# Packing an attention output of 28-of-32 rows to 448 rows, and running FF2 and the output product in pairs of 64-row halves, in a fused attention and MLP kernel

## The chip, the cores and the metric

The kernel runs on one core of one Trainium2 chip. The metric is the device time of one execution in microseconds (us). The engines of a core work side by side, each through its own stream of instructions in order: TensorE (PE) multiplies matrices, VectorE (DVE), ScalarE (ACT) and GpSimd (POOL) work on elements, SyncE (SP) and POOL issue transfers here. They wait for each other by semaphores. A matmul has a stationary operand, loaded by an instruction of its own (PEld), and a moving one; the result adds up in one of eight banks of PSUM.

## The reference

```
x = A_x                                   # (1, 2048, 448), bf16
xn = layernorm(x)
q, k, v = split(xn @ wqkv)                # 16 heads of 28
o[p] = softmax over 8 keys p, p-2, ..., p-14 of (q[p] . k) / sqrt(28), times v
s = concat_heads(o) @ wo                  # 448 x 448
g = silu(gelu(xn @ w1 + b1) @ w2 + b2)    # 448 -> 1792 -> 448
out = x + s * g
```

A position attends to eight positions at a distance of two, itself and earlier ones, so even and odd positions never meet.

## The kernel before

The 2048 positions are 16 tiles of 128, in 4 chunks (`NCH`) of 4 tiles (`TPC`); the even positions and the odd ones are laid out one after the other. All weights stay in SBUF. The kernel is a list of tasks, each a few instructions on one engine, and a string `ORDER` (L17 on) that names every task once, with a letter for its engine (P, V, A, G for POOL, S for SP, D for the landing of a transfer). `emit` goes through that string and issues the tasks, so the order on every engine is written out by hand; no scheduler moves anything. Buffers come out of pools (`take`, `give`) in the same order, and a task waits for whatever its data and its buffer depend on.

The stages:

- LayerNorm: statistics on DVE (L332, L336), the normalised tile `xn` (L366), which is transposed to `xnT` by PE (L381) for the first tiles and by transfers issued on SP (`dma_T`, L279) for the others. x is loaded by SP in transfers of four tiles (`x_sb`).
- qk and v projection (L457, L481) and FF1 (L516). D = 448 is three and a half times 128 rows, so these contract 7 slices of 64 rows. `pair(a, b)` runs two such jobs side by side, one in the top 64 rows of PE's array and the other in the bottom 64: first 4 slices of each, then 3 more with the halves exchanged, each job into its own bank. Between the two parts stands a "told" nop (L416) on POOL or SP: it waits for the first part's matmuls, and the second part waits for it. FF1's bias b1 comes by a transfer on POOL and is turned by PE (L772).
- The evacuated q and k are transposed by transfers on SP into `qkT` (L279); v is copied by transfers on POOL (L273).
- Scores (L599), exp on ACT (L609), the band masks (built on POOL, L731 to L738, multiplied on DVE, L615), values (L631). DVE brings the values' output into `oT` (L641, L645, L650, L655): four groups of 32 rows (a group is a head slot), of which 28 hold data, times 4 slices. `wo` is loaded in the same shape by POOL, with zeros in the rows that nothing fills.
- FF2: `ff2_part`, 14 full matmuls (128 rows by 448 columns) for each tile into one bank (L550); then y = bank + b2 on DVE (L565), tanh on ACT (L577; silu from the table for the last chunk, L572), and g on DVE (L581). g waits in a ring of buffers, which grows by the qkv weights' buffers (`late_g`) once those are spent.
- The end of a tile: `final_part`, 4 full matmuls with `wo` (L685), times g (L691, L693), plus x (L699), store by SP (L703).

PE's work around the end is FF2 of the last chunk and the output products, the last tile in column parts of 336 and 112.

Of the kernel before, what the change touches and what calls it, by code (L numbers as in the profile page):

```python
# [17 lines left out]
D0 V1 G17 S34 D35 A36 D37 V15 V16 P2 V22 S38 D39 V23 G50 V24 G51 D52 V25 V26 P3 V27 V28 S44 D45 V29 V30 G31 V18 V19  # L18
G32 P4 V20 G33 V21 S40 D41 P5 A53 S42 D43 P6 G100 S46 D47 P7 V60 P8 S48 D49 P9 V61 S76 D77 V64 A62 P10 S78 D79 V63
P11 P12 V106 P13 S80 D81 P14 V107 P108 V65 P109 A66 V110 P132 V67 V113 V114 P115 V117 A111 V68 D112 P136 P116 A118  # L20
P133 V69 A70 V71 S82 D83 V120 V121 S86 D87 P190 G102 V72 V73 A74 D119 P137 S88 D89 S90 D91 V191 P134 P122 P123 V124
P135 P138 A139 D125 P149 G150 A143 G168 D169 V75 V126 V127 V140 P128 G170 D171 P129 V130 A148 A54 G172 D173 P151
V153 D131 P318 G319 A145 P163 A152 G174 D175 V101 P320 S141 D142 A144 A321 A322 G178 D179 P156 S154 D155 V84 G176
D177 P313 V96 G164 P165 V85 P333 V97 V94 V95 V92 A167 G99 V200 V204 G314 P315 A166 G334 V205 P335 A316 V201 S202
D203 G157 V93 G98 S206 D207 P158 V196 V197 G180 D181 S198 D199 G182 D183 V192 V193 A336 P308 S194 D195 V160 A159
G309 A317 S146 D147 S161 D162 G184 D185 P323 G324 G186 D187 G188 D189 A337 P310 A311 S272 D273 V290 P325 P328 A326
G246 D247 V291 A327 P227 G329 P330 V294 V295 A331 S274 D275 V299 P215 G252 D253 G280 D281 V303 A312 G228 P229 A230
A231 A332 S276 D277 G216 P217 V301 A219 P338 G339 P548 P340 G549 P550 P234 G235 A341 V103 A218 A551 P208 A342 G104
P236 A237 A238 A552 V105 V296 P538 V304 P543 G539 G544 S232 D233 V300 P540 A542 G209 P210 P553 G554 A211 P545 S278
D279 A212 P533 G534 S220 D221 V302 S213 D214 A546 A547 P555 V305 V306 G307 V423 V419 V427 A541 A557 V428 P528 G529  # L30
P558 G559 A556 P535 A537 V431 P530 A532 P560 S239 D240 V432 V297 P222 A561 A531 A536 S433 D434 V292 G223 P241 V424
S429 D430 A562 S425 D426 P224 G242 P243 V293 G298 A225 A55 P691 A692 V420 G248 D249 A698 V355 S421 D422 V356 S357
D358 A694 G282 D283 G284 D285 P508 P509 P568 P569 A226 A696 P513 P518 V695 V693 V697 P514 V510 G286 D287 V343 G288
D289 V699 G250 D251 V351 V352 A511 A244 V245 G254 D255 V512 V570 V347 V348 V344 A571 V572 P700 V701 P519 V515 A516
P727 A728 S345 D346 V520 G256 D257 A521 G258 D259 V702 G260 D261 V705 A730 V706 A734 V707 G262 D263 V703 S349 D350
P523 V704 A732 V708 P524 P709 G264 D265 S353 D354 V517 A712 P359 A716 G266 D267 S360 P378 V713 V525 V522 A526 P361
A714 S379 A363 P380 A381 P366 S367 V362 S364 D365 V729 V717 G268 D269 A710 V711 P385 P368 A370 V715 V369 A382 S371
D372 S383 G270 D271 D384 V735 G386 P387 V388 P718 A389 V719 V720 V721 S390 D391 V722 P853 P745 V854 P573 V855 A748
V723 V724 A752 V527 V731 V725 V726 A746 V733 P858 P563 V859 P564 V565 P574 V575 P863 A566 V567 S856 D857 P736 G397
D398 V864 V865 P454 P461 G401 D402 V747 A750 S455 P456 P442 V737 A457 A458 G462 V741 V742 P463 P449 V743 V744 G443  # L40
V738 V739 S866 D867 A465 P444 S459 D460 V751 A464 A446 P435 V740 G450 S466 D467 V749 S436 V445 P451 A452 A453 P468
P437 V860 G469 V753 P470 V472 P754 P868 A438 A439 V471 S440 D441 V869 P763 S447 D448 A766 A770 V870 S871 D872 V755
A768 V756 P873 V874 A764 V757 V758 P578 P579 V580 V759 P781 A784 V767 V760 A786 S861 D862 P373 A581 A782 P583 S374
P375 G584 A788 A377 A56 V376 G407 D408 G409 D410 G411 D412 P585 V761 P588 P593 S594 S589 V762 G399 D400 V787 A586
P392 G415 D416 G405 D406 V582 V875 P595 V785 V771 A587 G393 P603 P590 G403 D404 A596 V769 A591 P394 S876 D877 G473
V396 A592 A395 G413 D414 V765 G417 D418 S604 G474 D475 G476 D477 G478 D479 P605 A607 P608 A576 P613 A597 A606 V789
P772 V777 S614 S609 P610 G480 D481 G482 D483 A611 A612 G484 D485 G486 D487 V773 P598 S599 P615 P600 A617 V778 V774
V783 P790 V775 V776 P878 V779 A602 V791 V780 G490 D491 A601 G488 D489 G494 D495 A616 A57 V879 V795 G492 D493 V792
V793 V796 P888 P799 A800 V889 A806 A802 A804 V577 P618 P619 V794 V890 V807 P883 V884 V805 P817 A824 V620 A820 P628
P835 A838 V801 A818 V803 V797 V798 P629 P808 V813 A836 P893 G496 D497 G498 D499 V630 P633 V814 V815 A621 A840 P623  # L50
V816 V825 V885 V622 A631 V632 P624 P634 S891 D892 A842 G500 D501 A822 A58 P643 P648 S644 V894 V895 S896 D897 P645
V635 P663 V841 A636 V843 V880 S881 D882 G502 D503 G504 D505 S649 V809 V625 V810 V811 V812 V823 A646 V837 A626 A647
V839 P650 S664 V819 P665 P638 A667 A666 V821 P653 A652 S639 A651 P640 S654 G506 D507 V637 P655 A657 A656 V627 S886
D887 A641 P826 V827 P668 S669 V828 V831 P658 S659 V829 V830 P670 A671 A642 P660 A661 V832 A672 A662 A59 V833 V834
P844 P903 V904 V905 S906 D907 P898 V899 P908 V909 V910 S911 D912 P918 P913 V845 V846 V847 V900 S901 D902 V848 V849
V850 V851 V852 P673 P674 V675 P681 P682 P923 P677 P678 P685 V683 A676 V914 V915 S916 D917 A684 V924 V925 S926 D927
V679 A680 P686 V919 V920 A687 S921 D922 P928 V929 V930 P688 P689 A690 S931 D932 P933 V934 V935 S936 D937
# [61 lines left out]
def kernel(  # L119
# [13 lines left out]
    P = 128  # L133
# [34 lines left out]
    const = ctx.enter_context(tc.tile_pool(name="const", bufs=1))  # L168
    psum = ctx.enter_context(tc.tile_pool(name="psum", bufs=1, space=bass.MemoryType.PSUM))
# [11 lines left out]
    wo = sb("wo", [P, KT, D])  # L181
# [21 lines left out]
    p_xn = ring("xn", 4, [P, 512])  # L203
# [11 lines left out]
    p_g.bufs = p_g.bufs + late_g  # L215
# [46 lines left out]
    t_wo = [plan.add("POOL", memset("gpsimd", wo[:], 0.0), [t_on])]  # L262
# [141 lines left out]
    def pair(a, b, early=False):  # L404
        held = {}

        def part(j, ps, kt, half, n):
            return lambda: j.part(ps, kt, half, n == 0, n == 6)

        def f1(k):  # L410
            p, q = buf(p_b, k, 0), buf(p_b, k, 1)
            held["last"] = together([part(a, p, kt, 0, kt) for kt in range(4)], [part(b, q, kt, 1, kt) for kt in range(4)])[-1]
        t = plan.add("PE", f1, a.deps + b.deps + a.late + b.late, take=(p_b, p_b) + a.into + b.into)

        def f2(k):
            held["told"] = (nc.gpsimd if k.on == "POOL" else nc.sync).nop()  # L416
# [116 lines left out]

    def ff2(t):
        t_g[t] = []
        for cs, n, end in parts(t):
            ff2_part(t, cs, n, end)

    def ff2_part(t, cs, n, end):
# [18 lines left out]
        a = halves[1]  # L558
        t_f2[t] = a

        if biased:
            y, pool, held = halves[0], p_b, ((p_b, halves[0], 0),)
        else:
            def f2(k):
                nc.vector.tensor_tensor(out=buf(p_y, k)[:, :n], in0=buf(p_b, halves[0])[:, :n], in1=b2[:, cs], op=ALU.add)  # L565
            y, pool = plan.add("DVE", f2, [a, t_b2], take=(p_y,), give=((p_b, halves[0], 0),)), p_y
# [3 lines left out]
        if c == NCH - 1:  # L570
# [15 lines left out]
    t_oT = [[] for _ in range(NT)]  # L586

# [88 lines left out]

    def final(t):
# [3 lines left out]
    def final_part(t, cs, n, g):  # L681
        def f1(k):
            ps = buf(p_b, k)
            for kt in range(KT):
                nc.tensor.matmul(ps[:, :n], oT[:, kt, t * P:(t + 1) * P], wo[:, kt, cs],  # L685
                                 start=(kt == 0), stop=(kt == KT - 1))
        a = plan.add("PE", f1, t_oT[t] + t_wo, take=(p_b,))

        def f2(k):
            if t >= NT - TPC:  # L690
                nc.vector.tensor_tensor(out=buf(p_sg, k)[:, :n], in0=buf(p_b, a)[:, :n], in1=buf(p_g, g)[:, :n], op=ALU.mult)  # L691
                return
            nc.vector.scalar_tensor_tensor(out=buf(p_sg, k)[:, :n], in0=buf(p_b, a)[:, :n], scalar=0.5,  # L693
                                           in1=buf(p_g, g)[:, :n], op0=ALU.mult, op1=ALU.mult)
        s = plan.add("DVE", f2, [a, g], take=(p_sg,), give=((p_b, a, 0), (p_g, g, 0)))
# [142 lines left out]
```

## Time and profile before

| | us |
|---|---|
| median of three runs | 155.57 |
| the three runs | 154.44, 155.7, 155.57 |
| the profiled execution | 155.02 |
| its span in the profile | 153.3 |

The profiled execution has 5268 instructions and moves 17.36 MB. The span is the time between the first and the last instruction on the core; 1.7 us of the execution lie around it. In the views below times count from the span's start. A row of the chain gives a start, a length, the engine and the line; a row of a group gives its busy time and the mean of one instruction in ns. PE's matmuls are pipelined, so the mean of one (342 ns for L550) is longer than the distance between two.

### The profile page before, as it was taken

The numbers are of one execution on the slowest core, as the hardware profiler recorded it, in microseconds if no ns is written. First come the engines' busy times: TensorE is split into PE (matmuls) and PEld (weight loads), VectorE is DVE, ScalarE is ACT, GpSimd is POOL, SyncE is SP. The second block draws the span as 40 slices with busy tenths as digits, with TensorE's granted clock in tenths as the row PEclk, the third lists the DMA queues.
The fourth block names the chain that finished last, engine by engine and source line by source line (L and its number), as shares of the span: only waits on it lengthen the run. The fifth ranks groups of instructions, "written<-read, shape, count | busy, mean of one in ns | idle before, by whom it ended". The sixth has DMA issues, their size and how long they took to land.

```text
span 153.3 us, 5268 instructions
## 1 busy us (share of the span) xinstructions
PE 148.6 (97%) x2200; PEld 78.6 (51%) x2200; DVE 107.3 (70%) x273; ACT 89.0 (58%) x165; POOL 43.0 (28%) x95
## 2 busy tenths in 40 slices
PE   6999999999999999999999999999999999999991
PEld 2454555555555555555554554445555445455561
DVE  4688540029524959899997877549977895989842
ACT  3239577786797407842246549689658358670320
POOL 7805666040349234020000005389600000000000
PEclk9999999999999999999999999999999999999999
DMA  4999988999997844069317681323310010002012
GB/s 150 285 287 330 155 164 178 156 375 176 285 122 141 122 87 88 4 128 129 85 34 137 75 106 46 96 59 88 92 34 0 4 62 30 4 32 62 13 47 60
DMA packets 33575, 17.36 MB, mean 113 GB/s; under 512 B 25203, under 2 KB 32387, under 8 KB 33552
## 3 DMA queue, kind: packets, MB, share of 16 engines
q1 hardware_dynamic: 31472, 14.03, 44.4%
q0 software_dynamic: 1936, 2.88, 8.9%
q8 instruction: 17, 0.28, 0.8%
q10 hardware_dynamic: 144, 0.11, 0.2%
q14 instruction: 6, 0.05, 0.1%
HBM read 7.06 MB, written 1.84 MB: 58 GB/s over the span
## 4 chain that ended last, share of the span: by engine, by line
PE 97%; DVE 1%; issue 0%; ACT 0%
PE bank L550 28%; PE bank L516 28%; PE bank L457 14%; PE bank L685 8%; PE bank L481 7%; PE bank L599 4%; PE bank L631 4%; PE bank L245 3%; PE bank L381 1%; DVE xnT L232 0%; DVE sg L691 0%; ACT w_in L572 0%; DVE h L237 0%; DVE o L699 0%; PE bank L548 0%
## 5 line engine op out<-in xcount | busy, mean ns | idle before, releaser
L516 PE MATMUL bank<-xnT,w 64*128 64x512 bf16 x392 | 45.1, 376 | 0.0
L550 PE MATMUL bank<-w,h 128*128 128x448 bf16 (+2 forms) x238 | 44.7, 342 | 0.0
L520 ACT ACTIVATE h<-bank,b 128x512 bf16<-128x512 f32 x56 | 35.4, 689 | 11.2 <-PE bank L516 11.2
L273 POOL DMA_DIRECT2D v<-v_tok x52 | 27.3, 533 | 48.6 <-DVE v_tok L232 25.3
L550 PEld LDWEIGHTS <-h 128*128 128x128 bf16 x238 | 22.1, 98 | 18.9
L516 PEld LDWEIGHTS <-w 64*128 64x128 bf16 x392 | 20.4, 94 | 20.9 <-issue 0.8
L457 PE MATMUL bank<-w_in,xnT 64*128 64x448 bf16 (+1 forms) x212 | 24.8, 352 | 0.2 <-DVE xnT L232 0.2
L609 ACT ACTIVATE E<-bank 128x456 bf16<-128x456 f32 (+1 forms) x36 | 17.8, 549 | 10.0 <-PE bank L599 9.3
L332 DVE BATCH_NORM_STATS2 st<-x_sb 128x6 f32<-128x448 bf16 x16 | 9.5, 609 | 12.7 <-DMA x_sb<-in_A_x_dram 12.7
L641 DVE STREAM_TRANSPOSE dt<-bank 128x480 f32<-128x480 f32 (+1 forms) x18 | 11.8, 663 | 7.0 <-PE bank L631 3.8
L457 PEld LDWEIGHTS <-xnT 64*128 64x128 bf16 (+1 forms) x212 | 10.9, 94 | 9.5 <-DVE xnT L232 0.4
L577 ACT ACTIVATE t<-y 128x448 f32<-128x448 f32 x12 | 6.9, 576 | 15.0 <-DVE y L565 15.0
L685 PE MATMUL bank<-wo,oT 128*128 128x448 bf16 (+2 forms) x68 | 14.1, 342 | 0.0
L481 PE MATMUL bank<-w_in,xnT 64*128 64x448 bf16 (+1 forms) x106 | 13.7, 352 | 0.0
L650 DVE STREAM_TRANSPOSE dt<-rd 128x480 f32<-128x480 f32 (+1 forms) x18 | 11.9, 666 | 0.3
L655 DVE TENSOR_TENSOR oT<-bank,dt 128x456 bf16<-128x456 f32 (+1 forms) x18 | 11.2, 628 | 0.4
L366 DVE TENSOR_SCALAR xn<-x_sb,mv,rstd 128x448 bf16<-128x448 bf16 x16 | 6.1, 398 | 7.1 <-POOL rstd L354 7.0
L565 DVE TENSOR_TENSOR y<-bank,b 128x448 f32<-128x448 f32 x15 | 9.2, 614 | 2.5 <-PE bank L550 2.4
L615 DVE TENSOR_TENSOR E<-E,m_gen 128x456 bf16<-128x456 bf16 x28 | 10.1, 385 | 0.5 <-ACT E L609 0.5
L230 ACT CAST qk_tok<-bank 128x448 bf16<-128x448 f32 x17 | 8.4, 536 | 1.6 <-PE bank L457 0.6
L685 PEld LDWEIGHTS <-oT 128*128 128x128 bf16 x68 | 6.0, 98 | 4.9
L481 PEld LDWEIGHTS <-xnT 64*128 64x128 bf16 (+1 forms) x106 | 5.8, 95 | 5.1 <-issue 0.2
(65 smaller groups left out, 121.3 us busy)
## 6 DMA issues: line engine op xcount, KB each, us to landing
out_dram<-o SPq DMA_DIRECT2D x15, 112.0 KB, 1.7
w<-in_B_w_dram SPq DMA_DIRECT2D x2, 784.0 KB, 7.3
w<-in_B_w_dram SPq DMA_DIRECT2D x2, 672.0 KB, 8.0
x_sb<-in_A_x_dram SPq DMA_DIRECT2D x3, 448.0 KB, 6.9
v<-v_tok POOLq DMA_DIRECT2D x20, 64.0 KB, 3.4
w_in<-in_A_wqkv_dram SPq DMA_DIRECT2D x3, 336.0 KB, 5.1
w<-in_B_w_dram SPq DMA_DIRECT2D x4, 112.0 KB, 7.3
wo<-in_A_wo_dram POOLq DMA_DIRECT2D x4, 98.0 KB, 4.4
```

Source lines behind the costliest of these rows:

```text
L273: nc.gpsimd.dma_start(dst(k), src())
L457: return nc.tensor.matmul(ps[:, :D], xnT[r, kt, cs], w, start=start, stop=stop)
L481: return nc.tensor.matmul(ps[:, :D], xnT[r, kt, k0:k0 + P], w, start=start, stop=stop)
L516: return nc.tensor.matmul(ps[:], w1[r, kt, ms], xnT[r, kt, cs], start=start, stop=stop)
L520: nc.scalar.activation(buf(p_h, own, i)[:], buf(p_b, own, i)[:], ACT.Gelu_apprx_tanh, bias=b1[:, mt:mt + 1])
L550: nc.tensor.matmul(ps[:, :n], buf(*h_at[(c, mt)])[:, j * P:(j + 1) * P], w2[:, mt, cs], start=(mt == 0 and not biased), stop=(mt == NMT - 1))
L609: nc.scalar.activation(buf(p_E, k)[:, :n], buf(p_b, a, hl)[:, :n], ACT.Exp, scale=SCALE)
L615: (nc.gpsimd if k.on == "POOL" else nc.vector).tensor_tensor(out=E[:, :n], in0=E[:, :n], in1=m[:, :n], op=ALU.mult)
L641: nc.vector.transpose(buf(p_dt, k)[:, :32 * m], buf(p_b, po, i)[:, :32 * m])
L650: nc.vector.transpose(buf(p_dt, d)[:, :32 * m].rearrange("p (b c) -> p b c", c=32), buf(p_rd, r)[:, :m].unsqueeze(2).to_broadcast((P, m, 32)))
L655: nc.vector.tensor_tensor(out=oT[:, :, q0:q0 + 2 * nq], in0=buf(p_b, po, i)[:, :n].rearrange("p (l q) -> p l q", l=4), in1=buf(p_dt, d)[:, ...
L685: nc.tensor.matmul(ps[:, :n], oT[:, kt, t * P:(t + 1) * P], wo[:, kt, cs], start=(kt == 0), stop=(kt == KT - 1))
```

## The change

1. FF2 of tiles 0 to 11 goes in pairs of tiles (`ff2_pair`, through `pair` with 14 and 14 half matmuls): one tile in the top 64 rows and the other in the bottom 64, exchanged after 14, with a told nop between. Tiles 12 to 15 stay as they were. What follows the matmuls is split off as `gate`.
2. The rows that hold data in `oT` become 448 of 512: a new `move` takes half of the last slice (64 rows) for two tiles at a time to a tile in DRAM by one transfer, and from there, by four transfers, into the unused four rows of the 32-row groups. All five are on SP. There are eight moves. For half of the tiles the bottom half of the last slice is moved away (`v` = 0), for the other half the top (`v` = 1).
3. The output product of tiles 0 to 11 goes in pairs of tiles, one of each kind (`final_pair`): 4 + 3 half matmuls instead of 4 full ones. Tiles 12 to 15 keep four full matmuls and read the packed layout. `wo` is therefore held twice; the second one lies in the buffers of `xn`, once all transposes have read them, and is loaded by SP. The store's part of `final_part` is split off as `store`.
4. The ring of g grows by eight more buffers, out of spent parts of `qkT`.
5. `ORDER` is new as a whole. Told nops: 30 on POOL and 19 on SP before, 40 and 21 after. Among the moves: the task that builds one band mask (G104) stands ahead of b1's memset and load (G50, G51) on POOL; SP issues the four xnT transposes, then x of tiles 8 to 11, both parts of w2 and x of tiles 12 to 15, ahead of the next qkT transpose; DVE has the statistics of tile 8 ahead of a qk evacuation.

```diff
-D0 V1 G17 S34 D35 A36 D37 V15 V16 P2 V22 S38 D39 V23 G50 V24 G51 D52 V25 V26 P3 V27 V28 S44 D45 V29 V30 G31 V18 V19
+D0 V1 G17 G104 S34 D35 A36 D37 V15 P2 V16 V22 S38 D39 V23 V24 G50 V25 V26 V27 P3 S44 D45 V28 V29 V30 G51 D52 V18 V19
...
-    wo = sb("wo", [P, KT, D])
+    xn_all = sb("xn", [P, 4, 512])
+    wo = [sb("wo", [P, KT, D]), xn_all[:, :, :D]]
...
+    spent_g = [qkT[:, w, g, :D] for w in range(2) for g in range(G)]
+    p_g.bufs = p_g.bufs + late_g + spent_g
...
-    t_wo = [plan.add("POOL", memset("gpsimd", wo[:], 0.0), [t_on])]
+    t_wo = [[plan.add("POOL", memset("gpsimd", wo[0][64:, 3, :], 0.0), [t_on])], []]
...
-    def pair(a, b, early=False):
+    def pair(a, b, early=False, n1=4, n2=3, after=(), give=()):
...
-            held["last"] = together([part(a, p, kt, 0, kt) for kt in range(4)], [part(b, q, kt, 1, kt) for kt in range(4)])[-1]
+            held["last"] = together([part(a, p, kt, 0, kt) for kt in range(n1)], [part(b, q, kt, 1, kt) for kt in range(n1)])[-1]
...
-            for i in together([part(b, q, kt, 0, kt + 4) for kt in range(3)], [part(a, p, kt, 1, kt + 4) for kt in range(3)])[0]:
+            for i in together([part(b, q, kt, 0, kt + n1) for kt in range(n2)], [part(a, p, kt, 1, kt + n1) for kt in range(n2)])[0]:
                 behind(i, held["told"])
-        u = plan.add("PE", f3, [told])
+        u = plan.add("PE", f3, [told] + list(after), give=give)
...
+    def ff2_pair(t):
+        c, j = divmod(t, TPC)
+
+        def job(t):
+            j = t % TPC
+
+            def part(ps, mt, half, start, stop):
+                r = half_rows(half)
+                return nc.tensor.matmul(ps[:, :D], buf(*h_at[(c, mt)])[r, j * P:(j + 1) * P], w2[r, mt, :], start=start, stop=stop)
+
+            def evac(a, own, i):
+                t_g[t] = []
+                gate(t, slice(0, D), D, a, own, i, False)
+            return _Job(D, part, [t_h[(c, mt)] for mt in range(NMT)] + t_w2[0] + t_w2[1] if t % 2 == 0 else [], evac)
+        last = j == TPC - 2
+        t_f2[t] = pair(job(t), job(t + 1), False, NMT, NMT, [t_f2[t - 2]] if last else (),
+                       tuple(h_at[(c, mt)] for mt in range(NMT)) if last else ())
...
+    def moved(v):
+        kept, gone = (0, 1), (2, 3)
+        if v:
+            kept, gone = gone, kept
+        return [x for k, h in zip(kept, gone) for x in ((h, 0, k, 4), (h, 16, h, 3))]
+
+    def move(v, ts):
+        cs = slice(ts[0] * P, (ts[-1] + 1) * P)
+        deps = [d for t in ts for d in t_oT[t]]
+        rest = dram.tile([64, len(ts) * P], BF16, name=f"rest{ts[0]}")
+
+        def out_fn(_):
+            nc.sync.dma_start(rest[:], oT[64 * (1 - v):64 * (1 - v) + 64, 3, cs])
+        a = plan.add("SP", out_fn, deps)
+        away = plan.add("DMA", lambda _: None, [a])
+        done = []
+        for h, c, g, n in moved(v):
+            def back_fn(_, r0=32 * (h % 2) + c, g=g, n=n):
+                nc.sync.dma_start(oT[32 * g + 28:32 * g + 32, :n, cs], rest[r0:r0 + 4 * n, :].rearrange("(k r) q -> r k q", r=4))
+            a = plan.add("SP", back_fn, [away])
+            done.append(plan.add("DMA", lambda _: None, [a]))
+        for t in ts:
+            t_oT[t] = t_oT[t] + done
...
+    def final_pair(t, u):
+        def job(t, v):
+            def part(ps, kt, half, start, stop):
+                r = half_rows(half)
+                return nc.tensor.matmul(ps[:, :D], oT[r, kt, t * P:(t + 1) * P], wo[v][r, kt, :], start=start, stop=stop)
+
+            def evac(a, own, i):
+                store(t, slice(0, D), D, a, own, i, t_g[t][0])
+            return _Job(D, part, t_oT[t] + t_wo[v], evac)
+        pair(job(t, 0), job(u, 1))
...
-        a = plan.add("PE", f1, t_oT[t] + t_wo, take=(p_b,))
+        a = plan.add("PE", f1, t_oT[t] + t_wo[0], take=(p_b,))
+        store(t, cs, n, a, a, 0, g)
...
-    t_wo += [dma("POOL", wo[32 * g:32 * g + 28, :, :], A_wo[112 * g:112 * g + 112, :].rearrange("(l c) d -> c l d", l=4),
-             [t_w2[1][0]] + t_wo[:1]) for g in range(G)]
+    def load_wo(v, eng, deps):
+        d = []
+        for g in range(G):
+            n = 4 if g // 2 == v else 3
+            d.append(dma(eng, wo[v][32 * g:32 * g + 28, :n, :],
+                         A_wo[112 * g:112 * g + 28 * n, :].rearrange("(l c) d -> c l d", l=n), deps))
+        for h, c, g, n in moved(v):
+            r0 = 112 * h + 84 + c
+            d.append(dma(eng, wo[v][32 * g + 28:32 * g + 32, :n, :], A_wo[r0:r0 + 4 * n, :].rearrange("(k r) d -> r k d", r=4), deps))
+        t_wo[v] += d
+    load_wo(0, "POOL", [t_w2[1][0]] + t_wo[0])
...
-        for t in range(c * TPC, (c + 1) * TPC):
-            ff2(t)
+    for t in range(0, NT - TPC, 2):
+        ff2_pair(t)
+    for t in range(NT - TPC, NT):
+        ff2(t)
...
+    t_wo[1].append(plan.add("POOL", memset("gpsimd", wo[1][:64, 3, :], 0.0), [t_xT[t] for t in range(TPC, NT)]))
+    load_wo(1, "SP", list(t_wo[1]))
+    for c in range(NCH):
+        move(0, (c * TPC, c * TPC + 1))
+        move(0 if c == NCH - 1 else 1, (c * TPC + 2, c * TPC + 3))
+    for t in range(0, NT - TPC, TPC):
+        final_pair(t, t + 2)
+        final_pair(t + 1, t + 3)
+    for t in range(NT - TPC, NT):
+        final(t)
```

More of the change, by code (lines that the diff above doesn't have):

```diff
@@ L23 @@
[L23 to L32, printed above, removed]
@@ L168 @@
     const = ctx.enter_context(tc.tile_pool(name="const", bufs=1))
+    dram = ctx.enter_context(tc.tile_pool(name="dram", bufs=1, space=bass.MemoryType.DRAM))
     psum = ctx.enter_context(tc.tile_pool(name="psum", bufs=1, space=bass.MemoryType.PSUM))
@@ L201, in ring @@
         return _Pool([sb(f"{name}{i}", shape, dt) for i in range(n)])
-    p_xn = ring("xn", 4, [P, 512])
+    p_xn = _Pool([xn_all[:, i, :] for i in range(4)])
     p_st = ring("st", 4, [P, 6], F32)
@@ L557, in ff2_part, with gate @@
                 halves.append(plan.add("PE", f1, [t_h[(c, mt)] for mt in range(7)] + t_w2[0] + ([t_row0, t_b2] if biased else []), take=(p_b,)))
-        a = halves[1]
-        t_f2[t] = a
+        t_f2[t] = halves[1]
+        gate(t, cs, n, halves[1], halves[0], 0, biased)
+    def gate(t, cs, n, a, own, i, biased):
         if biased:
-            y, pool, held = halves[0], p_b, ((p_b, halves[0], 0),)
+            y, pool, held = own, p_b, ((p_b, own, i),)
         else:
             def f2(k):
-                nc.vector.tensor_tensor(out=buf(p_y, k)[:, :n], in0=buf(p_b, halves[0])[:, :n], in1=b2[:, cs], op=ALU.add)
-            y, pool = plan.add("DVE", f2, [a, t_b2], take=(p_y,), give=((p_b, halves[0], 0),)), p_y
+                nc.vector.tensor_tensor(out=buf(p_y, k)[:, :n], in0=buf(p_b, own, i)[:, :n], in1=b2[:, cs], op=ALU.add)
+            y, pool = plan.add("DVE", f2, [a, t_b2], take=(p_y,), give=((p_b, own, i),)), p_y
             held = ((p_y, y, 0),)
         after = [a, y]
-        if c == NCH - 1:
+        if t >= NT - TPC:
             def silu(k):
@@ L684, in f1, with store @@
             for kt in range(KT):
[L685 removed]
+                nc.tensor.matmul(ps[:, :n], oT[:, kt, t * P:(t + 1) * P], wo[0][:, kt, cs],
                                  start=(kt == 0), stop=(kt == KT - 1))
[L687 removed]
+        a = plan.add("PE", f1, t_oT[t] + t_wo[0], take=(p_b,))
+        store(t, cs, n, a, a, 0, g)
+    def store(t, cs, n, a, own, i, g):
         def f2(k):
             if t >= NT - TPC:
[L691 removed]
+                nc.vector.tensor_tensor(out=buf(p_sg, k)[:, :n], in0=buf(p_b, own, i)[:, :n], in1=buf(p_g, g)[:, :n], op=ALU.mult)
                 return
[L693 removed]
+            nc.vector.scalar_tensor_tensor(out=buf(p_sg, k)[:, :n], in0=buf(p_b, own, i)[:, :n], scalar=0.5,
                                            in1=buf(p_g, g)[:, :n], op0=ALU.mult, op1=ALU.mult)
[L695 removed]
+        s = plan.add("DVE", f2, [a, g], take=(p_sg,), give=((p_b, own, i), (p_g, g, 0)))
         def f3(k):
@@ L763, in project @@
             t = plan.add("POOL", None, done)
-            t.slots[p_g] = list(range(len(p_g.free), len(p_g.bufs)))
+            t.slots[p_g] = list(range(4, 4 + len(late_g)))
             t.give = tuple((p_g, t, i) for i in range(len(late_g)))
@@ L802 @@
         values_sum(b)
-    for t in range(NT):
+    t = plan.add("POOL", None, [seen[b][0][0].deps[0] for b in range(2)])
+    t.slots[p_g] = list(range(len(p_g.bufs) - len(spent_g), len(p_g.bufs)))
+    t.give = tuple((p_g, t, i) for i in range(len(spent_g)))
+    t_wo[1].append(plan.add("POOL", memset("gpsimd", wo[1][:64, 3, :], 0.0), [t_xT[t] for t in range(TPC, NT)]))
[7 more added lines that the diff above has]
+    for t in range(NT - TPC, NT):
         final(t)
```

76 lines of the change are left out of this document (45 added, 31 removed).

## The prediction, made before the changed kernel had run

> **What bounds the kernel now.** I read the busy table and the granted clock first, then busy time by stretch, then the chain of work that ended last, then what the queues wait for.
>
> ```profile
> PE 148.6 (97%) x2200; PEld 78.6 (51%) x2200; DVE 107.3 (70%) x273; ACT 89.0 (58%) x165; POOL 43.0 (28%) x95
> PEclk9999999999999999999999999999999999999999
> PE 97%; DVE 1%; issue 0%; ACT 0%
> ```
> ```profile
> 0.00:11.30 11.30, 9.88 (x52) 4.72 (x54) 7.64 (x39) 3.73 (x9) 6.37 (x23) 1.00 0.83 240
> 11.30:150.00 138.70, 138.69 (x2152) 73.87 (x2146) 99.03 (x233) 85.12 (x157) 36.59 (x72) 1.00 0.53 105
> ```
>
> TensorE (PE) is 97% of the chain at a granted clock of 1.00, and from 11.3 us to 150 us it is busy for 138.69 of 138.70 us. So a matmul slot saved is time saved, any wait of PE that the change creates is time lost, and no other engine's busy time counts unless PE runs out of work behind it. The chain (start, length, what) gives the price of a slot:
>
> ```profile
> 45.65 9.38 PE bank L550 x49
> ...
> 61.08 5.40 PE bank L457 x56
> ...
> 68.64 1.43 PE bank L550 x7
> 70.07 0.76 PE bank L685 x4
> ...
> 84.22 0.61 PE bank L631 x64
> 84.82 0.86 PE bank L685 x4
> ...
> 133.81 3.89 PE bank L685 x20
> ```
>
> A full FF2 matmul (L550, 128 rows by 448 columns) takes 9.38/49 = 0.191 us, a full one of the output product (L685) 0.76/4 = 0.190. L457 is the qk projection in 64-row halves, two side by side: 56 matmuls are 28 pairs, 5.40/28 = 0.193 us each. A pair of halves thus costs what one full matmul costs, and does as much work. At 70.07 the output product follows full matmuls, at 84.82 the small ones of the values (L631, 64 rows by 32): its four take 0.86 instead of 0.76, so a change of shape costs 0.10 us.
>
> **The change part by part.**
>
> *Output product.* Tiles 0 to 11 have four full matmuls each now, 48 slots; as six pairs of tiles with 4 + 3 half slots they have 42. Six slots at 0.190: **-1.14 us**. Tiles 12 to 15 keep four. This is the only arithmetic that goes.
>
> *FF2 in pairs.* Fourteen full slots for each tile become 28 half pairs for two tiles: 12 x 14 = 168 slots on both sides. At 0.193 against 0.191 that is at most 168 x 0.002 = +0.3 us, at least 0, since 0.193 still holds a change of shape (0.10 over 28 pairs is 0.004). I take 0. The weight loads double in number, and they bear on a rival below:
>
> ```profile
> L550 PEld LDWEIGHTS <-h 128*128 128x128 bf16 x238 | 22.1, 98 | 18.9
> L516 PEld LDWEIGHTS <-w 64*128 64x128 bf16 x392 | 20.4, 94 | 20.9 <-issue 0.8
> ```
>
> A half load takes 94 ns, a full one 98: two half loads are 188 ns beside a slot of 190, so they just hide, as they do in the 0.193 of L457. The Trainium skill ("TensorE: Matmul & The Clock Gate", section "LDWEIGHTS (loading the stationary operand)") puts a load at columns/1.2 ns whatever its rows, 107 ns here, so that a half costs as much as a whole; a slot would then last 213 ns and 168 slots would add 3.9 us, an estimate from that page. The trace bears out that rows hardly matter (94 against 98) but not the figure: pairs at 193 ns leave no room for two loads of 107.
>
> *Changes of shape.* Counted along the built order of instructions, PE goes from full rows to halves or back some 40 times before and 37 after: 3 x 0.10 = **-0.3 us**.
>
> *The start.* A task that builds one mask on GpSimd (POOL) now stands ahead of b1's memset and load.
>
> ```profile
> 1.82 0.66 POOL L266 DMA_DIRECT2D b1r<-in_B_b_dram  x1 [0.30 <-POOL b1r L237]
> ```
> ```profile
> 31.58 0.19 POOL L731 MEMSET m<- 128x112 bf16 x1 [5.55 <-PE bank L457]
> ...
> 33.31 0.24 POOL L738 TENSOR_SCALAR_AFFINE_SELECT m<-m 64x56 bf16<-64x56 bf16 x1
> ```
> ```profile
> b1r<-in_B_b_dram POOLq DMA_DIRECT2D x1, 3.5 KB, 4.8
> ```
> ```profile
> L772 PE MATMUL bank<-ident,b1r x1: 219/219/219, 8.5 to 8.5; 128*128 128x128 bf16 x1
> ```
>
> The mask took 31.58 to 33.55, 1.97 us. The load, issued at 1.82 before, goes to 3.8 and lands 4.8 later at 8.6; its matmul ran at 8.5. PE has gaps until 11.3 (9.88 of 11.30 busy) that may take it up: between 0 and +0.2, **+0.1 us**.
>
> *x of tiles 8 to 11.* SyncE (SP) now issues this load behind four xnT transposes instead of two qkT transposes further on, so earlier, but DVE's order puts the statistics of tiles 8 and 10 around the evacuation of a qk bank that PE takes again at about 30 us (adding up slots along the built order).
>
> ```profile
> 18.59 5.43 SPq L279 DMA_TRANSPOSE xnT<-xn  x4
> ...
> 25.50 1.28 SPq L279 DMA_TRANSPOSE qkT<-qk_pair  x1
> 26.83 1.48 SPq L266 DMA_DIRECT2D x_sb<-in_A_x_dram  x2
> ```
> ```profile
> 33.33 0.63 DVE L332 BATCH_NORM_STATS2 st<-x_sb 128x6 f32<-128x448 bf16 x1 [11.67 <-DMA x_sb<-in_A_x_dram]
> ```
> ```profile
> xnT<-xn SPq DMA_TRANSPOSE x12, 3.8
> ...
> qkT<-qk_pair SPq DMA_TRANSPOSE x6, 5.1
> ```
>
> Before, DVE waited 11.67 us for x at no cost. There x was there at 33.33, 6.5 us after its issue, or 2.7 after the transpose ahead of it had landed (25.50 + 5.1 = 30.6). In the new order it is issued at about 24.0 (18.59 + 5.43): by the first reading it lands at 30.5, by the second at 22.7 + 3.8 + 2.7 = 29.2 (22.7 being the fourth transpose's issue). The bank is late when x lands after some 29.3: 0 to +1.2 us. I take the second reading, since the DMA queues are full there, and a third of the span between: **+0.4 us**.
>
> *Packing.* Eight moves, each one transfer of 64 rows by 256 columns (32 KB) to memory, and four back of four partitions each; eight loads for the second wo. All are on SP.
>
> ```profile
> 95.87 0.33 SPq L703 DMA_DIRECT2D out_dram<-o  x1
> ```
> ```profile
> 64.78 3.14 SPq L279 DMA_TRANSPOSE qkT<-qk_pair  x2
> 68.02 4.17 SPq L279 DMA_TRANSPOSE qkT<-qk_tok  x2
> 72.28 0.53 SPq L703 DMA_DIRECT2D out_dram<-o  x1
> ...
> 79.39 1.24 SPq L279 DMA_TRANSPOSE qkT<-qk_pair  x1
> 80.75 6.40 SPq L279 DMA_TRANSPOSE qkT<-qk_tok  x2
> ```
> ```profile
> SPq L416 <- PE bank L516: 30.3, 10, 12.0
> ...
> SPq L416 <- PE bank L457: 11.6, 4, 4.8
> ```
>
> 48 issues at 0.33 to 0.53 are 16 to 25 us more of SP, none of it on PE's path by itself. What can reach PE is the told nop (L416): between the two halves of every pair, POOL or SP waits for the first half's matmuls, and the second half waits for that. SP has 19 such nops before, 21 after; POOL 30 and 40. Before, SP stood waiting at them, 42 us in all, so they cost nothing. In the new order those of a qk pair and a v pair in the middle third stand behind a qkT transpose, and moves stand among them. Between the halves of those two pairs PE has three or four slots of another pair, 0.6 to 0.8 us, to cover the nop; a transpose takes SP 1.24 us when undisturbed. Bounds: 0, and the long transposes of the rival below. I take **+0.2 us**, near the undisturbed end, because SP stood waiting, so was early, at the 14 nops in the last two rows, of 19.
>
> *The end.* The order of the last tiles is the same in kind: FF2 of the last 112 columns, silu, product, sum, store. 0. A pair holds two banks for 28 slots where a tile held one for 14; FF1 pairs already run so without a gap in PE. 0.
>
> Sum: -1.14 - 0.3 + 0.1 + 0.4 + 0.2 = **-0.74 us**. The profiled run took 155.02 us (its span of 153.3 and 1.7 around it), so it would read 154.3; the median of the three runs shown, 155.57, would become 154.8. I state the middle, **154.5**.
>
> **The rivals.**
>
> 1. *A told nop late on SP (slower).* 80.75 6.40 x2 shows a transpose that holds SP far longer than 1.24: one of the two at least 3.2. If the two nops behind transposes meet such ones, each is 3.2 - 0.8 = 2.4 us late for PE, 4.8 in place of my 0.2: 154.5 + 4.6 = 159.1; with one of them, 156.7. A nop costs from a hold of over 0.8 us on; two holds of 2.2 us make the kernel over 1% slower (2 x 1.4 - 0.2 = 2.6). For: SP is strictly in order, and gets 48 more issues between its transposes. Against: nops waited 2.9 us on the average (30.3 + 11.6 over 14). Half of this rival's chance ends beyond 1%.
> 2. *All of the gain (faster).* x lands by the second reading and no nop is late: -1.44, from 155.57 and 155.02 that is 153.6 to 154.1. For: both waits have a reading at nothing. Against: the margins, 0.1 us for x.
> 3. *Loads don't hide.* FF2's half loads alternate between two row halves of two tiles; if the 188 ns aren't hidden as in L457 (other banks, other operands) but stick out by 20 ns a slot: 168 x 0.02 = +3.4, 157.9. Against: L457 and L516 run in just this shape.
> 4. *The packing is late at the end.* Tiles 14 and 15 wait for the last move.
>
> ```profile
> L650 DVE STREAM_TRANSPOSE dt<-rd 128x480 f32<-128x480 f32 (+1 forms) x18 | 11.9, 666 | 0.3
> L641 DVE STREAM_TRANSPOSE dt<-bank 128x480 f32<-128x480 f32 (+1 forms) x18 | 11.8, 663 | 7.0 <-PE bank L631 3.8 <-ACT h L520 1.6 <-ACT E L609 1.6
> L655 DVE TENSOR_TENSOR oT<-bank,dt 128x456 bf16<-128x456 f32 (+1 forms) x18 | 11.2, 628 | 0.4
> L645 DVE RECIPROCAL rd<-dt 128x15 f32<-128x15 f32 (+1 forms) x18 | 4.2, 239 | 0.3
> ```
> ```profile
> out_dram<-o SPq DMA_DIRECT2D x15, 112.0 KB, 1.7
> ...
> v<-v_tok POOLq DMA_DIRECT2D x20, 64.0 KB, 3.4
> ```
>
> Between the last values matmul and tile 15's product PE has about 50 full slots and 14 of 336 columns, 50 x 0.19 + 14 x 0.14 = 11.5 us. The output of two half blocks takes DVE 2 x (0.66 + 0.67 + 0.24 + 0.63) = 4.4, the move two landings of 1.7 to 3.4 and five issues of 0.33 to 0.53: 5.1 to 9.5. That is 9.5 to 13.9 against 11.5: 2.0 early to 2.4 late; at the middle of the late part, 1.2, the time is 155.7. The Trainium skill ("DMA: Bandwidth & Descriptors", section "Anatomy of one DMA — SWDGE (gpsimd) path") gives each DMA some 2.0 us of fixed cost, mostly for the write's receipt, worst into HBM; the move would then land in 2 x 2.0 plus its issues, 5.7 to 6.7 us, and be in time, an estimate. The 1.7 of the stores here agrees.
>
> **How the numbers follow.** My forecast by itself spans 153.9 to 155.3 (the terms of 0.1, 0.4 and 0.2 between 0 and twice their size, from 155.3, the middle of the two bases). Chances: my forecast 0.42, rival 1 0.24, rival 2 0.22, rival 3 0.05, rival 4 0.07. About 1% (1.5 us) is what a measurement tells from no change: below 154.0 is faster, above 157.1 slower. Faster: most of rival 2 (0.19) and the low edge of the forecast (0.07), **0.26**. Slower: half of rival 1 (0.13), rival 3 (0.05), and 0.08 for several of the upper bounds together (x +1.2, a nop, the loads' +0.3, a late move), **0.26**. Same: **0.48**. The range goes from 153.2 (rival 2 and a further 0.4 of run to run difference; the three runs lie 1.3 apart) to 157.2 (rival 1 at a little more than one long transpose); above it lie about 0.15, below 0.05.
>
> **What would show it.** Right: the output product as 20 full matmuls (tile 15 in two column parts) and 84 half ones, FF2's 336 halves at 0.19 us a pair, PE without a gap but near 8.5 and 30 us. Wrong: idle before L550 or L516 with "SPq L416" or a transpose as what ended it (rival 1); L550's pairs over 0.20 us (rival 3); PE idle before the last output products with a move's DMA as releaser (rival 4); an idle stretch near 30 us ended by DVE behind x_sb (x term).

## The result, and the profile after

The changed kernel takes 156.01 us in the median of 18 runs, beside 154.85 us of the kernel before, also 18: the ratio is 1.0066, with a 95% interval of 1.0041 to 1.0091. It is slower, by 0.7%. The profiled execution took 156.29 us (155.02 before), its span is 154.5 us (153.3).

The page's busy table and its chain by engine, of the changed kernel:

```profile
PE 147.0 (95%) x2404; PEld 80.0 (52%) x2404; DVE 105.3 (68%) x271; ACT 89.9 (58%) x167; POOL 45.3 (29%) x100
PE 84%; DMA 7%; DVE 4%; POOL 2%; issue 1%; POOLq 0%; DVEq 0%; SPq 0%
```

PE is busy 1.6 us less than before, and yet the span is 1.2 us longer. The chain says where to look: DMA has 7% of it and POOL 2%, where PE alone had 97%. Busy time by stretch (columns as before the change: length, then busy time of PE, PEld, DVE, ACT, POOL):

```profile
0.00:11.30 11.30, 7.94 (x44) 3.70 (x44) 7.49 (x37) 3.32 (x8) 7.06 (x30) 1.00 0.85 248
11.30:150.00 138.70, 138.01 (x2345) 75.45 (x2344) 96.15 (x231) 86.27 (x158) 38.21 (x70) 1.00 0.53 110
```

PE now stands still at the start (7.94 of 11.30 us busy, 9.88 before) and for 0.7 us later on. What it waited for (engine, line, released by: total, times, longest):

```profile
PE bank L389 <- DVE xn L374: 1.0, 1, 1.0
PE bank L836 <- DMA b1r<-in_B_b_dram: 0.9, 1, 0.9
PE bank L465 <- DMA xnT<-xn: 0.6, 1, 0.6
```
```profile
PEld L836 <- POOL m L802: 1.3, 1, 1.3
...
PEld L465 <- SPq L424: 0.6, 1, 0.6
```

Three waits cost time: for b1, for a transposed tile, and for a told nop on SP (L424 is the nop's line now). The fourth, for the first normalised tile, did not last: PE's first transposes start at 5.72 us, 0.50 later than before, but the last matmul ahead of b1's starts at 8.21, where it started at 8.30. The chain shows the first (start, length, what):

```profile
2.79 0.21 POOL m L800
3.06 0.24 POOL m L802
3.35 0.21 POOL b1r L245
3.57 0.29 issue
3.86 5.49 DMA b1r<-in_B_b_dram
9.35 0.14 issue
9.48 0.22 PE bank L836
```

POOL builds the mask, then sets and loads b1; the load, issued at 3.86, lands 5.49 us later, and its matmul runs at 9.48, where it ran at 8.49 before: **0.99 us later**. PE's last matmul before it ends at 8.56 and PE then waits for 0.92 us.

The second and the third, in PE's timeline (start, length, what):

```profile
60.69 2.81 PE L465 MATMUL bank<-w_in,xnT 64*128 64x448 bf16 x28
64.07 0.93 PE L465 MATMUL bank<-w_in,xnT 64*128 64x448 bf16 x8 [0.57 <-DMA xnT<-xn]
```
```profile
81.79 0.74 PE L489 MATMUL bank<-w_in,xnT 64*128 64x448 bf16 x6
82.65 0.74 PE L465 MATMUL bank<-w_in,xnT 64*128 64x448 bf16 x6
```

28 halves are 14 slots, 14 x 0.189 = 2.65 us, so the next could have started at 63.34 and started at 64.07: **0.73 us**. Six are 3 slots, 0.57 us: 82.36 against 82.65, **0.29 us**. The 0.189 is that of the new pairs themselves, here one pair of output products and one of FF2, 14 slots each:

```profile
89.82 2.65 PE bank L550 x28
...
119.80 2.65 PE bank L732 x28
```

Where the tile came late from, in DVE's and SP's timelines:

```profile
54.21 0.68 DVE L692 STREAM_TRANSPOSE dt<-bank 128x480 f32<-128x480 f32 x1 [1.43 <-PE bank L682]
...
57.53 0.38 DVE L374 TENSOR_SCALAR xn<-x_sb,mv,rstd 128x448 bf16<-128x448 bf16 x1
57.83 0.62 DVE L706 TENSOR_TENSOR oT<-bank,dt 128x456 bf16<-128x456 f32 x1
58.37 0.17 DVE L379 COPY xn<-xn 128x64 bf16<-128x64 bf16 x1
```
```profile
58.57 3.37 SPq L287 DMA_TRANSPOSE xnT<-xn  x2
```

Tile 12's normalisation (L374, L379) stands on DVE behind the output of two half blocks of values, whose first instruction waited 1.43 us for PE. Its transpose could be issued at 58.57 and landed 5.45 us later. Before, the four transposes of these tiles were issued from 41.97 us on:

```profile
41.97 6.01 SPq L279 DMA_TRANSPOSE xnT<-xn  x4
```

For the told nop, SP's timeline after the change:

```profile
77.14 0.84 SPq L627 DMA_DIRECT2D rest<-oT  x1
...
79.36 1.51 SPq L287 DMA_TRANSPOSE qkT<-qk_tok  x1
82.28 0.26 SPq L633 DMA_DIRECT2D oT<-rest  x1
```
```profile
SPq L633 <- DMA rest<-oT: 1.3, 1, 1.3
```

A move's transfer back (L633) waited 1.3 us on SP for the same move's transfer out (L627), and the nop stood behind it.

The ledger closes. From b1's matmul to the last instruction of DVE it is 150.71 - 8.49 = 142.22 us before and 151.69 - 9.48 = 142.21 after (the rows of DVE's last instruction are `150.49 0.22` and `151.47 0.22`). So behind the start the change gained and lost the same. The two traces show what, if the time is added up from the start of each group of PE's matmuls to the start of the next, from b1's matmul to the last one:

| us | before | after | difference |
|---|---|---|---|
| output products | 12.58 | 10.93 | -1.65 |
| FF2 | 43.14 | 43.25 | +0.11 |
| qk and v projection | 30.80 | 32.03 | +1.23 |
| scores | 5.71 | 6.11 | +0.40 |
| the rest | 49.10 | 49.00 | -0.10 |

The projection holds the two waits of 0.73 and 0.29 us. Without these and the scores the differences come to some -1.4 us, where -1.44 was forecast for slots and shapes. The busy time of the scores shows the same +0.4, first before, then after:

```profile
L599 PE MATMUL bank<-qkT 32*64 32x57 bf16 (+1 forms) x576 | 6.3, 200 | 0.0
```
```profile
L650 PE MATMUL bank<-qkT 32*64 32x57 bf16 (+1 forms) x576 | 6.7, 201 | 0.0
```

What is left of the difference is the 0.99 us of the start (and 0.2 us behind DVE's end).

### The profile page after: what moved, and what is told of

The parts are those of the page before. It is cut to its first block, busy times and chain, and to the rows that moved or that the text cites. A ratio compares the mean times of both kernels' runs of the same rounds, so it can differ in the third digit from the quotient of the medians.

```text
span 154.5 us, 5764 instructions
## 1 busy us (share of the span) xinstructions
PE 147.0 (95%) x2404; PEld 80.0 (52%) x2404; DVE 105.3 (68%) x271; ACT 89.9 (58%) x167; POOL 45.3 (29%) x100
## 4 chain that ended last, share of the span: by engine, by line
PE 84%; DMA 7%; DVE 4%; POOL 2%; issue 1%; POOLq 0%; DVEq 0%; SPq 0%
PE bank L524 28%; PE bank L550 18%; PE bank L465 11%; PE bank L489 7%; PE bank L576 7%; PE bank L732 5%; PE bank L682 4%; DMA b1r<-in_B_b_dram 4%; DMA xnT<-xn 4%; PE bank L650 3%; PE bank L747 1%; DVE sg L755 1%; DVE dt L692 1%; POOL m L802 0%; POOL m L800 0%
## 5 line engine op out<-in xcount | busy, mean ns | idle before, releaser
L524 PE MATMUL bank<-xnT,w 64*128 64x512 bf16 x392 | 46.3, 376 | 0.0
L550 PE MATMUL bank<-w,h 64*128 64x448 bf16 x336 | 33.9, 349 | 0.0
L524 PEld LDWEIGHTS <-w 64*128 64x128 bf16 x392 | 21.4, 94 | 19.3 <-issue 0.3
L465 PE MATMUL bank<-w_in,xnT 64*128 64x448 bf16 (+1 forms) x212 | 26.6, 350 | 0.9 <-DMA xnT<-xn 0.6
L550 PEld LDWEIGHTS <-h 64*128 64x128 bf16 x336 | 17.0, 94 | 13.1
L465 PEld LDWEIGHTS <-xnT 64*128 64x128 bf16 (+1 forms) x212 | 10.5, 94 | 10.4 <-DMA xnT<-xn 1.0
L489 PE MATMUL bank<-w_in,xnT 64*128 64x448 bf16 (+1 forms) x106 | 13.6, 349 | 0.0
L374 DVE TENSOR_SCALAR xn<-x_sb,mv,rstd 128x448 bf16<-128x448 bf16 x16 | 6.2, 408 | 10.8 <-POOL rstd L362 10.7
L576 PE MATMUL bank<-w,h 128*128 128x448 bf16 (+2 forms) x70 | 11.4, 315 | 0.0
L238 ACT CAST qk_tok<-bank 128x448 bf16<-128x448 f32 x14 | 7.0, 535 | 7.0 <-PE bank L465 6.7
L732 PE MATMUL bank<-wo,oT 64*128 64x448 bf16 x42 | 9.2, 349 | 0.0
L732 PE MATMUL bank<-xn,oT 64*128 64x448 bf16 x42 | 9.2, 349 | 0.0
```

The lines of the kernel that those rows point to most:

```text
L465: return nc.tensor.matmul(ps[:, :D], xnT[r, kt, cs], w, start=start, stop=stop)
L489: return nc.tensor.matmul(ps[:, :D], xnT[r, kt, k0:k0 + P], w, start=start, stop=stop)
L524: return nc.tensor.matmul(ps[:], w1[r, kt, ms], xnT[r, kt, cs], start=start, stop=stop)
L550: return nc.tensor.matmul(ps[:, :D], buf(*h_at[(c, mt)])[r, j * P:(j + 1) * P], w2[r, mt, :], start=start, stop=stop)
L576: nc.tensor.matmul(ps[:, :n], buf(*h_at[(c, mt)])[:, j * P:(j + 1) * P], w2[:, mt, cs], start=(mt == 0 and not biased), stop=(mt == NMT - 1))
L732: return nc.tensor.matmul(ps[:, :D], oT[r, kt, t * P:(t + 1) * P], wo[v][r, kt, :], start=start, stop=stop)
```

## The experiments

Each ratio is to the kernel before, run on the same chip, with its 95% interval. The difference of two such ratios has an interval of some 0.003 to 0.004 either way (0.5 to 0.6 us), worked out from theirs. "Order" is the string of tasks.

**b1 first.** The order of the changed kernel with b1's memset (G50) ahead and the mask (G104) behind b1's load:

```diff
-G17 G104 S34 ... V24 G50 V25 ... G51 D52 V18
+G17 G50 S34 ... V24 V25 ... G51 D52 G104 V18
```

> The changed kernel with b1's memset and load ahead of the mask on POOL, as before the change. Theory of the waits: b1 lands about 2 us earlier, PE's gap before the b1 transpose (9.48 us in the changed kernel, 8.49 before) closes, and 0.97 us comes back: about 155.0 us, ratio to the kernel before about 1.000. Rival (packing traffic or the half pairs carry the loss, PE catches the start up later): no more than 0.3 us comes back, ratio 1.005 or more.

Measured: 0.9987 (0.9969 to 1.0005), 154.51 us; 0.0079 or 1.2 us come back, so the rival falls. The b1 load is issued at 1.8 us, lands 4.0 us later, and its matmul runs at 8.1 us without a wait. That is 1.3 us earlier than 9.48, and a little earlier than in the kernel before (8.49). This one edit undoes the whole loss. Part of that may be luck: in this trace the other two waits are shorter too (0.26 us for 0.73, 0.13 for 0.29), although nothing there was edited.

**Tile 12 first.** Tile 12 is normalised in the place of tile 13, its transpose issued 40 tasks earlier:

```diff
-G315 V431 A694 ... D189 V706 V428 S631 S429 D430 P729
+G315 V427 A694 ... P386 V436 V428 S429 D430 V695 ... D189 V706 S631 P729
```

(V431, tile 13, takes V427's old place.)

> The changed kernel with tile 12 normalised in the place of tile 13, and its transpose to xnT issued about 45 instructions of the order earlier. Theory of the waits: the gap of 0.73 us before the qk projection of tile 12 (at 63.15 us) closes: ratio about 1.002. Rival (the transposes are slow for the traffic, wherever they stand): the gap stays, or moves to the next user of a transposed tile, ratio 1.006.

Measured: 1.0034 (1.0010 to 1.0059), 155.29 us. The transpose is issued at 52.48 us instead of 58.57, and PE's gap before that pair is gone. 0.0032 or 0.5 us come back; the interval of that difference takes in the 0.73, and nothing too, so what shows that this wait can be removed is the trace. The nop's wait of 0.29 us, which was not edited, is gone from this trace as well.

**All three waits.** Both edits, and the told nop of the qk pair (S451) ahead of the transfer back (S887):

```diff
-S398 D399 S887 D888 A461 ... V753 S451 P452
+S398 D399 A461 ... V753 S451 S887 D888 P452
```

> Both edits, and the told nop of the qk pair of tile 13 on SP ahead of the move's transfer back that stood before it. Theory of the waits: 0.97 + 0.73 + 0.28 = 1.98 us come back, 154.0 us, ratio about 0.994, so faster than the kernel before by some 0.9 us. Rival (other costs of the change, score matmuls and tail, grow as PE comes earlier): ratio 0.998 to 1.002.

Measured: 0.9953 (0.9927 to 0.9978), 154.09 us: faster than the kernel before. Of 1.98 us, 0.0113 x 154.9 = 1.75 came back. Its profile has a new wait: a told nop of FF2 that stands behind a long transpose on SP.

```profile
85.62 2.37 SPq L287 DMA_TRANSPOSE qkT<-qk_pair  x1
```
```profile
88.11 2.82 PE L550 MATMUL bank<-w,h 64*128 64x448 bf16 x28 [0.40 <-SPq L424]
```

**The mask first, in the kernel before.** The reverse, with nothing else of the change:

```diff
-D0 V1 G17 S34
+D0 V1 G17 G104 S34
```

> The kernel before with one edit: the same mask built ahead of b1's memset and load on POOL. Theory of the waits: the b1 transpose on PE runs about 1 us later and nothing takes that up: ratio 1.006, 155.8 us. Rival (the gaps of PE up to 11.3 us take it up): ratio 1.000 to 1.001.

Measured: 1.0157 (1.0124 to 1.0190), 157.64 us: both expectations fall, it costs 2.4 us and not 1.0. The six runs lie apart: two took 156.3 and 156.4 us, four 157.6 to 157.8, three of these four at a granted clock of 0.986 to 0.989. The profile, of one of the shorter two, shows a second effect. In DVE's timeline before, then DVE's and POOL's of this kernel:

```profile
4.77 0.40 DVE L366 TENSOR_SCALAR xn<-x_sb,mv,rstd 128x448 bf16<-128x448 bf16 x1
```
```profile
4.68 2.13 DVE L366 TENSOR_SCALAR xn<-x_sb,mv,rstd 128x448 bf16<-128x448 bf16 x1
```
```profile
4.96 1.58 POOL L237 MEMSET wo<- 128x1792 bf16 x1
```

DVE's first normalisation takes 2.13 us (0.40 in the kernel before) and ends 0.27 us after POOL's memset of wo, which the mask has pushed onto it. PE's first transposes then start at 6.86 instead of 5.22 us. The profiled run took 156.40 us, 1.4 more than that of the kernel before, which is what the traces account for: b1's matmul runs at 9.86 instead of 8.49 us. What the four longer runs spent 1.2 us more on isn't shown.

**The same with the memset out of the way.** G33, wo's memset, goes behind the other masks.

> The kernel before with the mask ahead of b1's load (ratio 1.0157), and wo's memset of 1.58 us moved behind the other masks on POOL. Theory (the memset held up DVE's first normalisation, 2.13 us in place of 0.40, and PE with it): that instruction takes 0.4 us again, PE starts its first transposes 1.5 us earlier, and what is left is b1's wait of about 1 us: ratio 1.005 to 1.008. Rival (DVE's 2.13 us has another cause, x's arrival or the masks): ratio 1.014 or more.

Measured: 1.0073 (1.0045 to 1.0101), 156.11 us; the normalisation takes 0.40 us again, and b1's matmul waits 0.99 us for its load and runs at 9.28.

```profile
4.98 0.40 DVE L366 TENSOR_SCALAR xn<-x_sb,mv,rstd 128x448 bf16<-128x448 bf16 x1
```
```profile
PE bank L772 <- DMA b1r<-in_B_b_dram: 1.0, 1, 1.0
```

So there are two costs: the mask ahead of b1's load is 0.0073, or 1.1 us, by itself, and the memset under the normalisation comes on top: 0.58 us in the two traces (b1's matmul at 9.86 instead of 9.28), more in the medians, with the four long runs in them. The two do not add up: in the kernel with both, b1's matmul has no wait of its own, as its load, issued at 3.86 us, had landed 5.9 us later, just before PE got there. The changed kernel hardly paid the second: its memset of wo is 0.47 us, and its first normalisation took 0.65 us.

**FF2 whole again**, on the version with the three waits mended (its ratio is 0.9953). `pair` gets a number of whole matmuls:

```diff
+        def full(j, ps):
+            return [j.part(ps, kt, 2, kt == 0, kt == whole - 1) for kt in range(whole)]
...
+            if whole:
+                held["last"] = full(a, p)[-1:]
+                return
...
+            if whole:
+                behind(full(b, q)[0], held["told"])
+                return
```

> The version with the three waits mended (ratio 0.9953 to the kernel before), with FF2 of tiles 0 to 11 as full matmuls again in the same tasks: 14 of one tile, told nop, 14 of the other. Theory: a pair of halves costs what a full matmul costs, so no change but a few changes of shape: ratio 0.995 to 0.997. Rival (half loads stick out, 20 ns a slot): 3.4 us faster, ratio 0.973.

Measured: 1.0026 (1.0002 to 1.0050), 155.15 us: 1.1 us slower than in pairs. The rival, that half loads stick out, is out. But it is more than the expected few changes of shape. Counted in the traces from 10 us on, PE changes its shape 45 times instead of 36, at 0.1 us each 0.9 us. That profile also has a wait of 0.7 us in the scores, which the view of waits puts down to issue, and the base has its 0.55 us at a nop, so these about cancel. From b1's matmul to the last one the two traces differ by 0.56 us only (141.87 and 141.31), so that the changes of shape make up the whole 1.1 us is argued, not shown.

**The output product whole**, on the same base, by the same means in `final_pair`.

> The same base, with the output product of tiles 0 to 11 in 4 full matmuls a tile in the same tasks, the packed rows and both layouts of wo kept: 48 slots in place of 42. Theory (PE sets the time, six slots at 0.19 us): 1.1 us slower, ratio 1.002 to 1.003. Rival (the slots saved were spent in waiting for the packing anyway): ratio 0.995 to 0.997.

Measured: 1.0117 (1.0083 to 1.0150), 156.61 us: 2.5 us slower, where 1.1 were expected. The chain of this kernel in one stretch:

```profile
97.96 0.65 PE bank L533 x6
98.61 0.86 PE bank L741 x4
99.47 0.75 PE bank L533 x6
100.23 1.62 PE bank L741 x8
101.85 0.97 PE bank L533 x8
```

and of its base, with the same tasks:

```profile
99.11 0.76 PE bank L732 x8
99.87 0.65 PE bank L524 x6
100.52 1.32 PE bank L732 x14
101.84 0.86 PE bank L524 x8
```

Between FF1 pairs (L533 and L524 are the same line of the two) each visit of full matmuls costs 0.10 going in and 0.10 going out: 0.86 for four, 0.75 and 0.97 for FF1 in place of 0.65 and 0.86. The traces have 53 changes of shape instead of 36: 17 x 0.10 = 1.7, with 1.1 for the six slots 2.8. That takes the slots as free of any wait for the packing, and the traces bear it out: the output products take 12.92 us whole and 10.93 in pairs, and FF1 around them, without the wait at the nop, 0.7 us more.

**No packing.** All 40 transfers are left out, on the same base.

> The same base, with all 40 transfers of the packing left out (the rows they would fill hold something else, so the output product of all tiles is incomplete). Theory: off PE's path except for told nops behind them on SP, of which the profile of the base shows one of 0.55 us at 87 us: ratio 0.992 to 0.995. Rival (the packing's traffic slows transposes and loads widely): ratio 0.988 or less.

Measured: 0.9947 (0.9925 to 0.9968), 153.97 us, against 0.9953. The difference is within its interval, so the traffic of the packing costs the base no more than about 0.6 us. In this trace the scores still take 6.01 us, so the packing isn't what made them longer.

**Four nops on POOL**, in place of SP (S401, S451, S463 and S649 become G401, G451, G463 and G649).

> The same base, with four told nops of the middle third (qk of tile 13, FF2 of tiles 6 and 7, v of tiles 10 and 11, and one more v pair) on POOL in place of SP. Theory (nops stand behind moves on SP): the gap of 0.55 us at 87 us goes, and the variation of runs with it: ratio 0.992 to 0.994. Rival (POOL's v copies hold them as long): 0.995 to 0.998.

Measured: 0.9986 (0.9956 to 1.0017), 154.38 us: not better than 0.9953, and its runs spread more, 153.7 to 156.1. The theory's numbers fall; that POOL's copies hold these nops is the expectation of the rival, but the profiled run, at 153.87 us, shows no such wait, so this isn't shown.

**One nop ahead of a transpose.** On the base of the three waits, the qkT transpose of the profile above goes behind the nop:

```diff
-S455 D456 A788 ... P648 S649
+A788 ... P648 S649 S455 D456
```

> The version with the three waits mended (ratio 0.9953), with one qkT transpose (tile 13, read by scores much later) issued behind the told nop of FF2 of tiles 6 and 7 instead of ahead of it. Theory (a nop stands behind a transpose that may hold SP for 2.4 us, as at 85.62 us of that profile): the gap of 0.55 us before that pair cannot come, 0.2 to 0.5 us on the average of runs: ratio 0.992 to 0.994. Rival (that gap was one run's): 0.995 again.

Measured: 0.9928 (0.9904 to 0.9953), 153.98 us. This is the lowest ratio of a version with the whole change in it: faster than the kernel before, and by 0.0138 or 2.1 us faster than the changed one. That this last edit did anything isn't shown: 0.0025 is less than the interval of the difference. In the trace of "The output product whole", which has the order of the base, the same transpose takes 1.30 us and PE has no gap behind it, which speaks for the rival:

```profile
85.58 1.30 SPq L287 DMA_TRANSPOSE qkT<-qk_pair  x1
```

## Why the prediction was wrong

The forecast was a gain of 0.74 us, and the kernel lost 1.2. That 156.01 us still lies in the range of 153.2 to 157.2 is luck: the upper part of the range stood for nops behind long transposes on SP, and the one nop that came late stood behind a transpose of 1.51 us and a transfer that waited. By its own steps:

- **Output product, -1.14.** Right in size and place. Its half pairs take 2.65 us for 14 slots, and with the changes of shape around them the output products take 1.65 us less. Undoing it in the new order costs 2.5 us: the six slots and the changes of shape that came with whole matmuls between FF1 pairs.
- **FF2 in pairs, 0.** Right for the slots: 28 halves take 2.65 us. The rival of loads that don't hide, and the estimate of 213 ns a slot made from the Trainium skill ("TensorE: Matmul & The Clock Gate", section "LDWEIGHTS (loading the stationary operand)"), are out: slots are 189 ns beside two loads of 94. In the new order, though, the pairs are worth 1.1 us, of which the count of changes of shape would give 0.9.
- **Changes of shape, -0.3.** Over the whole of the traces there are 40 before and 37 after, as counted, and the price of 0.10 us came out. But these are all changes of tile shape, those into and out of scores and values too; between full rows and halves, as the prediction words it, there are 28 before and 4 after.
- **The start, +0.1. This step failed.** It forecast that the gaps before 11.3 us "may take it up". They lay ahead of b1's matmul. In the kernel before, the 1.42 us of idle time in that stretch are two waits, which end at 1.25 and at 6.00 us, and from there PE is busy without a break:

```profile
PE bank L245 <- DVE eps_t L237: 1.2, 1, 1.2
PE bank L457 <- DVE xnT L232: 0.2, 1, 0.2
```

A wait that starts at 8.56 us has nothing behind it that can give. And the load landed at 9.35, not at 8.6, since it took 5.49 us and not 4.8: the landing time was taken from a single row, of a load issued 2 us earlier, and all four loads of b1 that were issued at 3.9 us took 5.3 us or more. It cost 0.99 us in the trace; 1.2 came back in the experiment, 1.1 were lost by the same move in the kernel before.
- **x of tiles 8 to 11, +0.4.** It cost nothing: x was there at 28.25 us, ahead of both readings.

```profile
28.25 0.63 DVE L340 BATCH_NORM_STATS2 st<-x_sb 128x6 f32<-128x448 bf16 x1 [6.46 <-DMA x_sb<-in_A_x_dram]
```

- **Packing, +0.2.** 0.29 in the profiled run (0.13 and nothing in two others with this part unchanged), at one of the two nops named, though by a move that waits for its own first half and not by a transpose. Rival 1's mechanism, a long transpose of 2.37 us ahead of a nop, came in the version with the three waits mended; the last experiment, which took that nop out from behind it, ended at 0.9928, where 0.9953 had been, a difference within its interval.
- **A term that wasn't there, +0.73.** The sum put the late transposes at nothing without a reason: the prediction went through SP's and DVE's order around 30 us but not through the transposes of the last four tiles, which the new order moves from 42 us to between 58 and 71 us, on DVE behind work that waits for PE.
- **The scores, +0.4.** Not foreseen, and not explained; the cause stays open: four of the nine groups of 64 take 0.04 to 0.16 us more than the 0.63 of the others, and the sum stays up in every version of the changed kernel. With the packing's transfers left out they still take 6.01 us, so these aren't the cause. That the term of x, +0.4, did not come and this one did is a cancellation by chance.
- **The end, and rival 4: 0.** No wait of PE for a move's landing appears. The rival's second estimate used the Trainium skill's figure for transfers that GpSimd issues ("DMA: Bandwidth & Descriptors", section "Anatomy of one DMA — SWDGE (gpsimd) path"). The moves are issued on SP: there the last move's first transfer back was issued 1.8 us behind its transfer out (140.85 and 142.62 us), another's in the middle of the kernel 5.1 us behind (77.14 and 82.28).

So the gain is there as it was worked out, six slots and some changes of shape; less the 0.4 of the scores it is 1.0 us, and the two versions with the waits mended are 0.7 and 1.1 us faster than the kernel before. The sign came from work that the new order put late: one mask, one normalisation and one nop, the mask above all.

## What to carry to other kernels

Where one engine is busy for 138.69 of 138.70 us, a rewrite of the order is a larger risk than the edit that it carries: go through every task that moved, by engine, and ask when its last input can land and what the bound engine has left to do until then. Idle time ahead of a wait can't pay for that wait; only what lies behind it can. Count the changes of shape along the order before pricing an edit by its slots, and keep a nop that the bound engine waits for ahead of transfers that nobody needs soon.

## What the hardware did that was not expected

- A memset of 1.58 us on POOL made a DVE instruction of 0.40 us last 2.13, until just behind the memset's end. The Trainium skill ("SBUF — State Buffer", section "Who interferes with whom") says that a DVE instruction that uses both ports and one of GpSimd exclude each other for a whole instruction, and that issue order decides who waits. The trace agrees with the wait for the other's end; DVE's record begins 0.28 us ahead of the memset's, so the order of issue isn't what it shows, nor does it show which ports the instruction uses. In the kernel before, the same memset, 2.91 to 4.49 us, ran beside a statistics instruction on DVE that took its usual 0.63.
- A load of 3.5 KB took 3.6 to 5.9 us to land in the twelve traces. In the eight that issue it at 1.8 us it took 3.6 to 4.8 (4.8 in the kernel before, 4.0 with b1 first), in the four that issue it at 3.9 us 5.3 to 5.9 (5.49 in the changed kernel, 5.9 with the mask first in the kernel before). The later issues are the longer ones.
- A move's transfer out of 32 KB, issued from 77.14 us, was still waited for at 82.2, some 5 us, where the one store of 28 KB on the same queue, the last of the kernel before, landed in 1.4 us.
